# Two late output stores moved from SyncE's queue to GpSimd's queue in a dilated-convolution kernel

## The chip, the cores and the metric

The kernel runs on one core of a Trainium2 chip. The metric is the device time in microseconds of one execution; the median of the runs is compared.

## The reference

A gated causal convolution with three taps and dilation 2, followed by a projection, on `x` of 2 x 16000 x 256, `w` of 3 x 256 x 512 and `w_o` of 256 x 256, all in bf16:

```
xp = jnp.pad(x, ((0, 0), (4, 0), (0, 0)))
h = x @ w[0] + xp[:, 2:2 + T] @ w[1] + xp[:, 0:T] @ w[2]     # taps at t, t-2, t-4
f, g = h[..., :256], h[..., 256:]
z = tanh(f) * sigmoid(g)
out = z @ w_o
```

## The kernel before, in words

Time is cut into groups of rows. A wide group holds 256 rows of 8 time steps (the first wide ones 128 rows), and is worked in four blocks of 128 output channels of `h`. For each block TensorE multiplies sums and differences of shifted inputs with prepared weights (the function `mm`), ScalarE and VectorE put the partial results together, ScalarE takes tanh and sigmoid, VectorE multiplies both to `z`. Then `out_mm` projects a piece of `z` (128 rows, two time steps each, 2 x 256 columns in PSUM), a copy on ScalarE or VectorE brings it to a bf16 tile `osb` in SBUF, and a store takes it to `out`. All this is written out in one order by hand (`tc.manual_schedule()`), so the order of the text is the order on each engine.

In the middle of the kernel two pieces share one store of 256 KB, issued on SyncE's queue by `store` (L391). At the end, from the last four pieces of the group before on, every piece has a store of its own, 128 KB. The last group has eight pieces: (row block 0 or P, jp 0 to 3). `out_mm` writes them into `G["o", rb0, jp]`. `last_evict` (L665) takes two of them: it copies the first with ScalarE and the second with VectorE into the two halves of one `osb`, and issues one store after each copy (L675), on the queue that its argument `queues` names for it. With `split` the second piece is copied in two halves, one on each engine.

In the text below the eight stores at L675 are named by their place: in the order of the program these are N1 and N2 (row block 0, jp 1 and 2, L693), N3 and N4 (row block P, jp 1 and 2, L695), A1 and N5 (row block 0, jp 0 and 3, L696), N6 and A2 (row block P, jp 0 and 3, L699). N1, N3, A1 and N6 follow a copy by ScalarE, N2, N4 and N5 one by VectorE, and A2 the two half copies. A1 and A2 are issued from ScalarE's queue, the six N from SyncE's.

After the last of them SyncE waits at L725 for the completion of all transfers; then the engines meet in a closing barrier.

Of the kernel before, what the change touches and what calls it, by code (L numbers as in the profile page):

```python
# [13 lines left out]
def kernel(  # L14
# [23 lines left out]
    nc = tc.nc  # L38
# [4 lines left out]
    P = 128  # L43
# [621 lines left out]
    def last_evict(rb0, jps, queues, split=False):  # L665
        osb = osb_pool.tile([P, 2, 2, D], bf16, name="osb")
        rows = out[b, t0 + 8 * rb0:t0 + 8 * (rb0 + P), :].rearrange("(p j) d -> p j d", j=8)
        at = [rows[:, 2 * jp:2 * jp + 2, :] for jp in jps]
        for i, (jp, copy) in enumerate(zip(jps, (nc.scalar.copy, nc.vector.tensor_copy))):
            if split and i:  # L670
                for q, half_copy in enumerate((nc.vector.tensor_copy, nc.scalar.copy)):
                    half_copy(out=osb[:, i, q], in_=G["o", rb0, jp][q])  # L672
            else:
                copy(out=osb[:, i], in_=G["o", rb0, jp])  # L674
            queues[i].dma_start(out=at[i], in_=osb[:, i])  # L675

    def last_mm(rb0, jps, where):
        two_pieces([(G, rb0, jp) for jp in jps], where)
# [11 lines left out]
    out_evict(*left[1][0], False, True)  # L690
    out_evict(*left[1][1], False, True)
    last_mm(P, (1, 2), "y")
    last_evict(0, (1, 2), (nc.sync, nc.sync))  # L693
    last_mm(0, (0, 3), "o")
    last_evict(P, (1, 2), (nc.sync, nc.sync))  # L695
    last_evict(0, (0, 3), (nc.scalar, nc.sync))  # L696
    out_mm(G, P, 0, new_y()[:, 0].rearrange("p (q d) -> p q d", q=2))
    out_mm(G, P, 3, [new_y()[:, 0, :D], ps_o.tile([P, D], f32, name="o_ps", tag="o_ps")[:]])
# [31 lines left out]
```

## Time and profile before

| | |
|---|---|
| median of 3 runs | 262.14 us (261.97 to 263.0) |
| the profiled execution: its own time | 261.54 us |
| the profiled execution: its span, first to last instruction | 259.8 us |
| TensorE busy | 254.9 us, 98% of the span |
| VectorE, ScalarE, GpSimd busy | 226.0, 246.1, 115.3 us |
| SyncE's and ScalarE's transfers (q1, q10) | 33.99 and 0.92 MB |

The busy times are sums over the span. In a row of the timeline the first number is the start in us from the span's start and the second the duration; SPq, ACTq and POOLq are the queues of SyncE, ScalarE and GpSimd, and a DMA_DIRECT2D on one of them is the issuing of a transfer, not its data. "DMA share" in a table of stretches is the mean busy share of the core's 16 DMA engines in that stretch, as their packet records give it (it can come out a little over 1).

### The profile page before, as it was taken

What the parts mean: (1) busy time and instruction counts of PE and PEld (TensorE: products, weight loads), DVE (VectorE), ACT (ScalarE), POOL (GpSimd) and SP (SyncE); (2) the same over time, 40 slices, a digit from 0 to 9 for tenths busy, and PEclk for the clock granted to TensorE, in tenths of its full rate; (3) what the DMA queues carried; (4) which work ended last, traced back from release to release, by engine and by line L of the source; (5) the groups of instructions that cost most, each with busy time, mean ns of one, the idle gap of its engine ahead of it and who ended that gap; (6) DMA issues with size and microseconds to landing.
All of it is one profiled execution on the core that took longest, in us unless ns stands there. A gap on an engine that the chain in (4) does not pass through costs nothing.

```text
span 259.8 us, 4299 instructions
## 1 busy us (share of the span) xinstructions
PE 254.9 (98%) x1491; PEld 146.0 (56%) x1491; DVE 226.0 (87%) x270; ACT 246.1 (95%) x378; POOL 115.3 (44%) x128
## 2 busy tenths in 40 slices
PE   8999999999999999999999999999999999999993
PEld 4577765555555555555555555555555555555572
DVE  2889999988988988999988988988988988986673
ACT  5768889999999999999999999999999999999993
POOL 1432435445445445446445445445445445444240
PEclk9999999999999999999999999999999999999999
DMA  7999782471925628283481925728294221221226
GB/s 199 208 196 213 150 203 81 113 207 50 252 81 125 171 85 210 82 178 116 129 208 40 252 83 111 182 87 209 81 153 142 82 81 43 81 83 43 81 101 222
DMA packets 79685, 35.17 MB, mean 135 GB/s; under 512 B 69552, under 2 KB 72368, under 8 KB 79664
## 3 DMA queue, kind: packets, MB, share of 16 engines
q1 hardware_dynamic: 78560, 33.99, 52.1%
q10 hardware_dynamic: 1104, 0.92, 1.4%
q8 instruction: 11, 0.18, 0.3%
q14 instruction: 10, 0.08, 0.1%
HBM read 1.18 MB, written 16.38 MB: 68 GB/s over the span
## 4 chain that ended last, share of the span: by engine, by line
PE 97%; DVE 0%; ACT 0%; issue 0%; DVEq 0%; ACTq 0%
PE y L259 70%; PE o_ps L374 19%; PE y L316 2%; PE e_ps L316 2%; PE y L149 1%; PE y L374 1%; PE f_ps L316 1%; PE wt_ps L170 0%; DVE osb L674 0%; ACT osb L674 0%; PE tp L182 0%; PE tq L182 0%; DVEq L725 0%; ACT osb L672 0%; DVEq L672 0%
## 5 line engine op out<-in xcount | busy, mean ns | idle before, releaser
L293 POOL TENSOR_TENSOR sv<-sv,st 128x512 f32<-128x512 f32 x60 | 76.5, 1275 | 17.4 <-ACT sv L290 7.9
L241 POOL TENSOR_TENSOR qd<-xq 128x256 bf16<-128x256 bf16 (+2 forms) x58 | 33.7, 585 | 111.4 <-DVE zw L349 54.5
L300 DVE TENSOR_TENSOR sv<-sv,y 128x1024 f32<-128x1024 f32 x60 | 72.7, 1212 | 4.0 <-PE y L259 3.8
L259 PE MATMUL y<-qd,wd_sb 128*128 128x512 bf16 (+1 forms) x256 | 61.6, 366 | 0.0
L411 ACT CAST osb<-o_ps 128x512 bf16<-128x512 f32 x114 | 61.1, 591 | 0.0
L374 PE MATMUL o_ps<-wo_sb,zw 128*128 128x256 bf16 x450 | 58.9, 273 | 0.0
L296 DVE SCALAR_TENSOR_TENSOR y<-st,y 128x512 f32<-128x512 f32 x60 | 41.8, 696 | 19.6 <-PE y L259 11.1
L374 PEld LDWEIGHTS <-zw 128*128 128x128 bf16 x480 | 46.9, 98 | 17.4
L259 PE MATMUL y<-qp,wmh_sb 128*128 128x512 bf16 (+1 forms) x128 | 45.0, 366 | 0.0
L259 PEld LDWEIGHTS <-wd_sb 128*128 128x128 bf16 x256 | 25.0, 98 | 27.4 <-issue 0.5
L221 DVE TENSOR_TENSOR q<-xq 128x2048 bf16<-128x2048 bf16 (+3 forms) x34 | 37.9, 1119 | 0.9 <-DMA xq<-in_x_dram 0.8
L290 ACT ACTIVATE sv<-y 128x512 f32<-128x512 f32 x60 | 35.9, 598 | 0.9 <-PE y L259 0.7
L286 ACT ACTIVATE st<-y 128x512 f32<-128x512 f32 x60 | 36.3, 606 | 0.2 <-PE y L259 0.2
L259 PE MATMUL y<-q,wu_sb 128*128 128x512 bf16 (+1 forms) x128 | 35.7, 366 | 0.0
L259 PE MATMUL y<-qm,wph_sb 128*128 128x512 bf16 (+1 forms) x128 | 35.7, 366 | 0.0
L259 PE MATMUL y<-q,wt_sb 128*128 128x512 bf16 (+1 forms) x128 | 35.7, 366 | 0.0
L259 PE MATMUL y<-qm,wm_sb 128*128 128x512 bf16 (+1 forms) x128 | 35.7, 366 | 0.0
L349 DVE TENSOR_TENSOR zw<-thw,sgw 128x2048 bf16<-128x2048 bf16 x28 | 34.1, 1218 | 0.0
L340 ACT ACTIVATE sgw<-sv 128x1024 bf16<-128x1024 f32 x30 | 32.3, 1078 | 0.7 <-DVE sv L300 0.5
L340 ACT ACTIVATE thw<-sv 128x1024 bf16<-128x1024 f32 x30 | 32.3, 1078 | 0.3 <-DVE sv L300 0.3
L340 ACT ACTIVATE sgw<-y 128x1024 bf16<-128x1024 f32 x30 | 31.3, 1044 | 0.0
L340 ACT ACTIVATE thw<-y 128x1024 bf16<-128x1024 f32 x30 | 31.3, 1043 | 0.0
(68 smaller groups left out, 179.9 us busy)
## 6 DMA issues: line engine op xcount, KB each, us to landing
out_dram<-osb SPq DMA_DIRECT2D x54, 256.0 KB, 2.1
out_dram<-osb SPq DMA_DIRECT2D x10, 128.0 KB, 1.9
w_sb<-in_w_dram ACTq DMA_DIRECT2D x2, 256.0 KB, 4.2
out_dram<-osb SPq DMA_DIRECT2D x2, 160.0 KB, 2.0
xq<-in_x_dram SPq DMA_TRANSPOSE x17, 6.7
osb<-in_x_dram SPq DMA_DIRECT2D x1, 256.0 KB, 2.5
w_sb<-in_w_dram SPq DMA_DIRECT2D x1, 256.0 KB, 3.8
out_dram<-osb ACTq DMA_DIRECT2D x2, 128.0 KB, 2.1
```

The lines of the kernel that those rows point to most:

```text
L221: ins = nc.vector.tensor_tensor(out=sums(G, "q")[:, h, :, :, :, sl].rearrange("p h q ct r -> p h (q ct) r"), in0=s, in1=a, op=ALU.subtract ...
L241: ins = after(eng.tensor_tensor(out=sums(G, "qd")[:, h, q, ct, sl], in0=a, in1=s, op=ALU.subtract), behind)
L259: nc.tensor.matmul(B.y[:, bank, i * n:(i + 1) * n], lhsT=wmat[:, ct, osl], rhs=mv[:, :, ct, :B.R], start=new and ct == 0 and i == 0, stop= ...
L286: nc.scalar.mul(B.st[:], B.y[:, 0, :], 4.0)
L290: nc.scalar.mul(B.sv[:, 0], B.y[:, 0, :], 2.0)
L293: after(nc.gpsimd.tensor_tensor(out=B.sv[:, 1], in0=B.sv[:, 0], in1=B.st[:], op=ALU.subtract), behind)
L296: nc.vector.scalar_tensor_tensor(out=B.y[:, 1, :], in0=B.st[:], scalar=-0.5, in1=B.y[:, 0, :], op0=ALU.mult, op1=ALU.add)
L300: nc.vector.tensor_tensor(out=B.sv[:], in0=B.sv[:], in1=B.y[:], op=ALU.subtract)
L340: nc.scalar.activation(out=dst[:, :, ph].rearrange("p b j c -> p j b c"), in_=at[:].rearrange("p j (b c) -> p j b c", b=hi - lo), func=fun ...
L349: return eng.tensor_tensor(out=z, in0=th, in1=sg, op=ALU.mult)
L374: nc.tensor.matmul(o_ps[q] if isinstance(o_ps, list) else o_ps[:, q, :], lhsT=z_columns(G, rb0, jp, q, dt), rhs=wo_sb[:, dt, :], start=(dt ...
L411: copy(out=G["osb"][:, 2 * h:2 * h + 2, :], in_=o_ps)
```

## The change

The first store of two pairs, N1 and N3, is issued from GpSimd's queue. Nothing else is changed in the text.

```diff
     last_mm(P, (1, 2), "y")
-    last_evict(0, (1, 2), (nc.sync, nc.sync))
+    last_evict(0, (1, 2), (nc.gpsimd, nc.sync))
     last_mm(0, (0, 3), "o")
-    last_evict(P, (1, 2), (nc.sync, nc.sync))
+    last_evict(P, (1, 2), (nc.gpsimd, nc.sync))
     last_evict(0, (0, 3), (nc.scalar, nc.sync))
```

On SyncE's queue these rows stand at the end of the last group; DMAHW0 to DMAHW7 are the completion counts that transfers of the two hardware queues take in turn, Activation and DVE the counts of finished instructions of ScalarE and VectorE.

```order
-L675 DMA out_dram<-osb 128x512 [waits DMAHW0_49,Activation_49]
-L675 DMA out_dram<-osb 128x512 [waits DMAHW1_49,DVE_49]
-L675 DMA out_dram<-osb 128x512 [waits DMAHW2_49,Activation_49]
-L675 DMA out_dram<-osb 128x512 [waits DMAHW4_49,DVE_49]
-L675 DMA out_dram<-osb 128x512 [waits DMAHW5_49,DVE_49]
-L675 DMA out_dram<-osb 128x512 [waits DMAHW7_49,Activation_49]
+L675 DMA out_dram<-osb 128x512 [waits DMAHW0_49,DVE_49]
+L675 DMA out_dram<-osb 128x512 [waits DMAHW2_49,DVE_49]
+L675 DMA out_dram<-osb 128x512 [waits DMAHW3_49,DVE_49]
+L675 DMA out_dram<-osb 128x512 [waits DMAHW5_49,Activation_49]
```

The two stores that waited for ScalarE's copies, N1 and N3, are gone; N2, N4, N5 and N6 are left in their order and use the counts one or two places earlier.

On GpSimd's queue this is the end of the program; `sv` and `zw` are the last block's partial sums and gated values.

```order
 L293 TENSOR_TENSOR sv<-sv,st 128x512 [waits Activation_49,Pool_49]
 L644 TENSOR_TENSOR zw<-thw,sgw 128x1024 [waits PE_49]
+L675 DMA out_dram<-osb 128x512 [waits Activation_49] x2
 L725 UNCONDITIONAL_BRANCH
 L725 ISA [waits barrier_Pool_Activation_PE_DVE_SP_gather]
```

The two stores stand behind GpSimd's last arithmetic instruction and ahead of its part of the closing barrier. The order on TensorE and VectorE is the same as before; on ScalarE only the numbers of the counts differ.

## The prediction

> **What bounds the kernel now.** I read the page first: what ends the kernel, and whether the DMA engines matter there.
>
> ```profile
> span 259.8 us, 4299 instructions
> PE 97%; DVE 0%; ACT 0%; issue 0%; DVEq 0%; ACTq 0%
> DMA  7999782471925628283481925728294221221226
> GB/s 199 208 196 213 150 203 81 113 207 50 252 81 125 171 85 210 82 178 116 129 208 40 252 83 111 182 87 209 81 153 142 82 81 43 81 83 43 81 101 222
> ```
>
> TensorE carries 97% of the chain, and the change touches nothing that TensorE waits for: only the last slice (222 GB/s over 6.5 us) can move. Next the issues by line, for the sizes, and the end in stretches, whose last two columns are DMA share and GB/s.
>
> ```profile
> out_dram<-osb SPq DMA_DIRECT2D x10, 128.0 KB, 1.9
> out_dram<-osb ACTq DMA_DIRECT2D x2, 128.0 KB, 2.1
> ...
> 254.00:255.00 1.00, 1.00 (x12) 0.90 (x10) 0.97 (x2) 1.00 (x2) 0.00 (x0) 1.00 0.79 262
> 255.00:256.00 1.00, 0.68 (x7) 0.36 (x4) 1.00 (x3) 0.57 (x3) 0.00 (x0) 1.00 0.82 269
> 256.00:258.00 2.00, 0.00 (x0) 0.00 (x0) 0.21 (x1) 0.34 (x2) 0.00 (x0) 1.00 1.03 340
> 258.00:258.30 0.30, 0.00 (x0) 0.00 (x0) 0.00 (x0) 0.00 (x0) 0.00 (x0) 1.00 0.95 318
> 258.30:259.80 1.50, 0.00 (x0) 0.00 (x0) 0.00 (x0) 0.00 (x0) 0.00 (x0) 1.00 0.01 3
> ```
>
> Two regimes. Until 256.0 the DMA engines have a fifth of their time free (0.79, 0.82). From 256.0 to 258.3 they are full at 340 GB/s, so a store of 128 KB (131,072 bytes) takes 0.386 us there. The rest, 1.5 us, is landing and closing. Now SyncE's queue in that time, from the timeline in narrow windows (start, duration of the issue).
>
> ```profile
> 252.68 1.30 SPq L391 DMA_DIRECT2D out_dram<-osb  x3
> 253.58 0.40 SPq L391 DMA_DIRECT2D out_dram<-osb  x1
> 254.07 0.41 SPq L675 DMA_DIRECT2D out_dram<-osb  x1
> 254.58 0.38 SPq L675 DMA_DIRECT2D out_dram<-osb  x1
> 255.06 0.40 SPq L675 DMA_DIRECT2D out_dram<-osb  x1
> 255.55 0.44 SPq L675 DMA_DIRECT2D out_dram<-osb  x1
> 256.08 0.41 SPq L675 DMA_DIRECT2D out_dram<-osb  x1
> 256.58 0.40 SPq L675 DMA_DIRECT2D out_dram<-osb  x1
> ```
>
> The last six rows are N1 to N6, one about every 0.5 us: 131,072 bytes in 0.5 us are 262 GB/s, the rate of the first regime, which the issuing sets. And the copies that release the stores, with ScalarE's own two issues.
>
> ```profile
> 253.22 0.62 ACT L674 CAST osb<-y 128x512 bf16<-128x512 f32 x1
> 253.97 0.59 ACT L674 CAST osb<-y 128x512 bf16<-128x512 f32 x1
> 255.07 0.36 ACTq L675 DMA_DIRECT2D out_dram<-osb  x1
> 255.48 0.59 ACT L674 CAST osb<-y 128x512 bf16<-128x512 f32 x1 [0.43 <-PE y L374]
> 256.37 0.36 ACTq L675 DMA_DIRECT2D out_dram<-osb  x1
> ...
> 253.86 1.42 DVE L674 CAST osb<-y 128x512 bf16<-128x512 f32 x2 [0.61 <-ACT osb L674]
> 254.59 0.69 DVE L674 CAST osb<-y 128x512 bf16<-128x512 f32 x1
> 255.20 0.68 DVE L674 CAST osb<-o_ps 128x512 bf16<-128x512 f32 x1
> 255.79 0.41 DVE L672 CAST osb<-y 128x256 bf16<-128x256 f32 x1
> ```
>
> N1 is ready at 253.22 + 0.62 = 253.84, N2 at 253.86 + 0.69 = 254.55, N3 at 253.97 + 0.59 = 254.56, N4 at 254.59 + 0.69 = 255.28, N5 at 255.20 + 0.68 = 255.88, N6 at 255.48 + 0.59 = 256.07. SyncE issues them 0.23, 0.03, 0.50, 0.27, 0.20 and 0.51 us later. That is the slack the change is about.
>
> **Why the end stands where it does.** Two more numbers: how long after its issue a store's data move, and what follows the data (the row of landings is that of the eight stores).
>
> ```profile
> 253.40:253.50 0.10, 0.10 (x3) 0.09 (x2) 0.00 (x0) 0.10 (x1) 0.00 (x0) 1.00 0.00 0
> 253.50:253.90 0.40, 0.40 (x6) 0.35 (x5) 0.04 (x1) 0.33 (x1) 0.00 (x0) 1.00 0.89 300
> ...
> DMA to landing us min/median/max: 1.9/2.1/2.4
> ...
> L725 SPq EVENT_SEMAPHORE  x3: 17/17/28, 258.9 to 259.7; - x3
> L725 SPq DRAIN  x3: 7/7/13, 259.0 to 259.3; - x3
> ```
>
> The store issued at 252.68 begins to move data at 253.5: 0.82 us. With that, first data come at 254.89 (N1), 255.40 (N2), 255.88 (N3), 255.89 (A1), 256.37 (N4), 256.90 (N5), 257.19 (A2), 257.40 (N6). N1 and N2 find idle engines. From N3 on, six stores stand back to back: 255.88 + 6 x 0.386 = 258.20, where the table shows the data ending at 258.3. The last landing is taken at 258.9, 0.6 us behind the data, and 0.9 us of closing lead to 259.8. So the kernel's end is the end of this DMA train plus 1.5 us.
>
> **The change part by part.** *SyncE loses two issues.* Nothing queued on it is held any more than by its own copy: N2 goes at 254.58, N4 at 255.30, N5 at 255.91, N6 when N5's 0.41 us and the gap of 0.09 seen between these rows are over, 256.41. Gains: 0, 0.25, 0.17 and 0.17 us. A1 and A2 stay at 255.07 and 256.37. The other completion counts cost nothing: each was last used by a store issued at 252.68 or before (N1 to N6 land 1.9 to 2.4 us after issue), and N6 issues 3.7 us after that.
>
> *What this is worth alone.* First data: N2 255.40, A1 255.89, N4 256.12, N5 256.73, A2 257.19, N6 257.23. If N1 and N3 were out of the way before 255.40, the floor would be A2 and N6 behind 257.19: 257.19 + 2 x 0.386 = 257.96, 0.24 us earlier than 258.20. That is the largest gain there is; the engines are full, and bytes are not removed.
>
> *GpSimd gains two issues.* The trace of before shows no DMA on its queue, so the price g of one is bounded by rows.
>
> ```profile
> 247.69 2.13 POOL L644 TENSOR_TENSOR zw<-thw,sgw 128x1024 bf16<-128x1024 bf16 x1
> ...
> L293 POOL TENSOR_TENSOR sv<-sv,st 128x512 f32<-128x512 f32 x60 | 76.5, 1275 | 17.4 <-ACT sv L290 7.9 <-DVE qm L232 5.5 <-DVE q L221 4.0
> ...
> L446 POOL TENSOR_TENSOR wph_sb<-sv,w_sb 128x1024 bf16<-128x1024 f32 x1 | 3.2, 3162 | 5.1 <-DVE sv L444 5.1
> ```
>
> The queue is free from 249.82 (247.69 + 2.13), 4 us before N1 is ready, so nothing there holds the stores and nothing but the barrier stands behind them. From below, g is SyncE's 0.40 us. From above it is the longest thing GpSimd does here, 3.16 us. I take 1.28 us, its usual price for one instruction on a 128x512 tile, as the nearest row of the same engine and shape; it is a choice, not a measurement. Behind the issue I keep SyncE's 0.82 - 0.40 = 0.42 us to the first data. Then N1 starts at 253.86, its data move at 253.86 + 1.28 + 0.42 = 255.56, and N3, which has been ready since 254.56 but stands behind N1, moves at 253.86 + 2 x 1.28 + 0.42 = 256.84.
>
> *The sum.* N1 now misses the idle time ahead of N2. From N2 on, all eight stores stand in one train without a gap: 255.40 + 8 x 0.386 = 258.49, against 258.20. That is +0.29 us. With g = 0.40, N1 is through at 255.07, N3 comes at 255.40 together with N2, and seven stores follow: 255.40 + 7 x 0.386 = 258.10, so -0.10 us. With g between about 1.1 and 1.5 the train is the same eight, and up to 1.8 a gap of a tenth comes into it; above that N3 itself is last: its landing is 253.86 + 2g + 0.42 + 0.386 + 0.6 = 255.27 + 2g, which reaches today's 258.9 at g = 1.82 and, at g = 3.16, 261.6: +2.7 us.
>
> The Trainium skill, "DMA: Bandwidth & Descriptors", section "Rules for kernel authors", says that transfers issued from SyncE, ScalarE and GpSimd run on the same 16 engines and interleave, so spreading them saves issue time only. The row of 340 GB/s agrees: the full stretch gains nothing from another queue. The page's "Specifications" give about 1 us to the first byte from GpSimd against 0.6 us from SyncE; by that estimate N1 would come 0.4 us later than by SyncE's rows, at 255.08, eight stores would end at 258.17, and the change would be worth nothing.
>
> **The sum against the runs.** On the profiled execution the span goes from 259.8 to 260.1 and its own time from 261.54 to 261.8. The median of the runs shown is 262.14, 0.6 above that execution; on it the forecast is 262.4 us. Half a per cent, 1.3 us, is about what a measurement of this kernel can tell from no change.
>
> **The rivals.** *GpSimd issues nearly as quickly as SyncE* (g up to 0.8). For it: its smallest rows are short and its queue is idle. Against it: no row shows it issuing anything. The time: -0.24 to 0, that is 261.9 to 262.1. Within half a per cent. Chance 0.14.
>
> *GpSimd's stores are slow, and N3 becomes the last to land.* This is the case on the other side: slower. The place is the wait at L725, the price twice g because N3 queues behind N1 on one in-order queue. It is slower by over 1.3 us when 255.27 + 2g exceeds 260.2, from g = 2.47 on, or when the first store, the first that this queue issues in the whole kernel, takes that much extra once. For it: 2.13 and 3.16 us rows on this engine, at double the tile; nothing has been issued there before. Against it: the 60 instructions on this tile's shape take 1.28. The time: 263.4 to 264.8. Chance 0.23.
>
> *VectorE holds GpSimd up while it copies.* VectorE's copies run almost without a break from 253.86 to 255.79 + 0.41 = 256.20. If GpSimd could prepare nothing beside them, both stores would start at 256.20: with g = 1.28 N3's data come at 256.20 + 2.56 + 0.42 = 259.18, end at 259.57, against 258.20: +1.4 us, 263.5; with g = 0.40 five stores from N5's 256.73 on end at 258.66, +0.5 us, 262.6. For it: the kernel itself orders GpSimd's arithmetic behind VectorE's (`after`, L92). Against it: that concerns instructions with two SBUF inputs; these copies have one input, in PSUM. Chance 0.09, half of it over the bound. The Trainium skill, "SBUF — State Buffer", section "SBUF: two separate sides", describes such a hold-up of GpSimd's transfers for VectorE's two-port modes; no run here shows it so far, and by its condition these copies would not cause it.
>
> *A gain of over half a per cent* finds no row: the floor is 0.24 us. I leave 0.03 for what the profile does not show.
>
> **How the numbers follow.** The forecast (g about 0.9 to 2.2, end moved by 0 to +0.8 us) has 0.51. Within half a per cent: 0.51 + 0.14 + 0.04 = 0.69, less 0.03 for runs that scatter upward = 0.66. Slower: 0.23 + 0.05 + 0.03 = 0.31. Faster: 0.03. The range goes from the floor's 261.9 less a tenth for scatter, 261.8, up to g = 3.16, 264.8; below it I leave the 0.03 and some scatter, above it a longer first issue.
>
> **What would show it.** Right: in the timeline N4, N5 and N6 issue on SPq at 255.3, 255.9 and 256.4; two DMA_DIRECT2D on POOLq, the first from 253.86, over 1 us each; the DMA share in 254 to 255 lower than 0.79, then full without a gap until about 258.5; the last landing at 259.2. Wrong: if a stretch with a low DMA share appears after 257 and the wait at L725 ends on one of GpSimd's two stores, the issue was slow (or, if it begins only after 256.2, held up by the copies); if the full stretch ends before 258.2, it was quick. Any difference ahead of 253 us is not from this change.

## The result and the profile after

The changed kernel takes 262.51 us (median of 22 runs, 261.95 to 263.59) against 262.02 us (22 runs, 261.35 to 263.0). The ratio is 1.0023, 95% interval 1.0014 to 1.0033: slower by about 0.6 us by the ratio (0.5 between the medians), inside the half per cent. The forecast was 262.4, the range 261.8 to 264.8.

The profiled execution after has a span of 261.4 us, 1.6 us more, and most of that lies ahead of the change. From the page, the chain of work that ended last:

```profile
span 261.4 us, 4298 instructions
PE 88%; DMA 4%; SPq 4%; issue 1%; DVE 1%; ACT 0%; DVEq 0%; ACTq 0%
```

In this execution the chain runs through waits for loads and through SyncE's queue, which the same instructions did not show before; ScalarE's first copy at L674 starts at 254.29 instead of 253.22. This part scatters from execution to execution (below). So the end is compared as a **tail**: from the start of that copy to the end of the span. It was 6.54 us (253.22 to 259.75, from the unrounded times); it is 261.40 - 254.29 = 7.11, or 0.57 more. To set a time after against one before, subtract 1.07.

The timeline of the tail, in narrow windows: ScalarE's first copy, GpSimd's two issues, SyncE's four (N2, N4, N5, N6), ScalarE's two.

```profile
254.29 1.34 ACT L674 CAST osb<-y 128x512 bf16<-128x512 f32 x2
255.22 0.71 POOL L675 DMA_DIRECT2D out_dram<-osb  x1 [4.32 <-ACT osb L674]
255.94 0.55 POOL L675 DMA_DIRECT2D out_dram<-osb  x1
255.66 0.33 SPq L675 DMA_DIRECT2D out_dram<-osb  x1
256.38 0.33 SPq L675 DMA_DIRECT2D out_dram<-osb  x1
256.98 0.33 SPq L675 DMA_DIRECT2D out_dram<-osb  x1
257.41 0.60 SPq L675 DMA_DIRECT2D out_dram<-osb  x1
256.15 0.36 ACTq L675 DMA_DIRECT2D out_dram<-osb  x1
257.50 0.36 ACTq L675 DMA_DIRECT2D out_dram<-osb  x1
```

N1 is ready at 254.29 + 0.62 = 254.91 (copy's duration as before) and its issue starts 0.31 us later. GpSimd then takes 0.71 us for it and 0.55 for N3. Now the DMA engines, share and GB/s in the last two columns, with one row of before at the matching place (255.02 + 1.07 = 256.09) ahead.

```profile
255.02:255.41 0.39, 0.39 (x7) 0.34 (x4) 0.39 (x2) 0.03 (x1) 0.00 (x0) 1.00 0.90 299
```

```profile
255.50:256.00 0.50, 0.50 (x7) 0.45 (x5) 0.47 (x2) 0.50 (x2) 0.49 (x2) 1.00 0.79 262
256.00:256.10 0.10, 0.10 (x3) 0.09 (x2) 0.10 (x1) 0.10 (x1) 0.10 (x1) 1.00 0.15 41
256.10:256.50 0.40, 0.40 (x7) 0.34 (x4) 0.40 (x2) 0.02 (x1) 0.39 (x1) 1.00 0.00 0
256.50:256.90 0.40, 0.26 (x3) 0.00 (x0) 0.40 (x2) 0.29 (x1) 0.00 (x0) 1.00 1.05 370
256.90:257.30 0.40, 0.00 (x0) 0.00 (x0) 0.39 (x2) 0.40 (x2) 0.00 (x0) 1.00 0.85 258
257.30:257.70 0.40, 0.00 (x0) 0.00 (x0) 0.00 (x0) 0.17 (x1) 0.00 (x0) 1.00 0.76 259
257.70:258.10 0.40, 0.00 (x0) 0.00 (x0) 0.00 (x0) 0.00 (x0) 0.00 (x0) 1.00 0.92 310
258.10:258.50 0.40, 0.00 (x0) 0.00 (x0) 0.00 (x0) 0.00 (x0) 0.00 (x0) 1.00 1.01 333
258.50:259.50 1.00, 0.00 (x0) 0.00 (x0) 0.00 (x0) 0.00 (x0) 0.00 (x0) 0.90 0.99 342
259.50:259.80 0.30, 0.00 (x0) 0.00 (x0) 0.00 (x0) 0.00 (x0) 0.00 (x0) 0.50 0.91 311
259.80:259.90 0.10, 0.00 (x0) 0.00 (x0) 0.00 (x0) 0.00 (x0) 0.00 (x0) 0.50 0.10 21
```

This is the main part: for 0.4 us, from 256.10 to 256.50, the 16 engines move nothing, where before they moved N1. N1's data come a little ahead of N2's, and all eight stores then stand in one train. The train is not full all the way: behind its first 0.4 us the share is 0.85, 0.76 and 0.92 until 258.10, and only then 1. By the packet records (each transfer's pieces, with their times) the data end 5.56 us after the first copy instead of 5.19: 0.38 us later. The rest of the 0.57 is in the closing: first SyncE's waits at L725, the last row of waits before, then after.

```profile
L725 SPq EVENT_SEMAPHORE  x1: 28/28/28, 258.9 to 258.9; - x1
L725 SPq DRAIN  x1: 13/13/13, 259.0 to 259.0; - x1
```

```profile
L725 SPq EVENT_SEMAPHORE  x3: 28/28/28, 260.4 to 260.5; - x3
L725 SPq DRAIN  x1: 13/13/13, 260.6 to 260.6; - x1
```

Before, the wait that N6's landing ended was the last of SyncE's list. Now N6 has an earlier completion count, two more waits stand behind it, at 0.06 us each, and SyncE goes on 0.12 us later. From there to the end of the span it took 0.75 us before and takes 0.81 now. Most of this is in one row of GpSimd's queue, which clears semaphores (the counters that the waits read): before, then after.

```profile
L725 POOLq EVENT_SEMAPHORE_RANGE_CLEAR  x1: 94/94/94, 259.4 to 259.4; - x1
```

```profile
L725 POOLq EVENT_SEMAPHORE_RANGE_CLEAR  x1: 138/138/138, 261.0 to 261.0; - x1
```

It takes 138 or 139 ns in every run below with a store on GpSimd's queue, and 94 to 96 in every run without one.

### The profile page after: what moved, and what is told of

It reads as the page before. It is cut to its first block, busy times and chain, and to the rows that moved or that the text cites. A ratio compares the mean times of both kernels' runs of the same rounds, so it can differ in the third digit from the quotient of the medians.

```text
span 261.4 us, 4298 instructions
## 1 busy us (share of the span) xinstructions
PE 255.9 (98%) x1491; PEld 146.3 (56%) x1491; DVE 225.3 (86%) x270; ACT 246.2 (94%) x378; POOL 116.2 (44%) x130
## 4 chain that ended last, share of the span: by engine, by line
PE 88%; DMA 4%; SPq 4%; issue 1%; DVE 1%; ACT 0%; DVEq 0%; ACTq 0%
PE y L259 67%; PE o_ps L374 19%; DMA xq<-in_x_dram 4%; SPq L128 3%; PE y L374 1%; PE f_ps L316 1%; SPq L114 1%; DVE sv L300 0%; PE e_ps L316 0%; DVE osb L674 0%; ACT osb L674 0%; SPq L145 0%; SPq L141 0%; DVEq L725 0%; ACT osb L672 0%
## 5 line engine op out<-in xcount | busy, mean ns | idle before, releaser
L221 DVE TENSOR_TENSOR q<-xq 128x2048 bf16<-128x2048 bf16 (+3 forms) x34 | 37.2, 1100 | 0.9 <-DMA xq<-in_x_dram 0.9
```

Of the source, the lines that this page charges most:

```text
L221: ins = nc.vector.tensor_tensor(out=sums(G, "q")[:, h, :, :, :, sl].rearrange("p h q ct r -> p h (q ct) r"), in0=s, in1=a, op=ALU.subtract ...
```

## The experiments

Every experiment keeps the kernel's arithmetic and moves stores, or cuts two of them in pieces, and nothing else. "First copy" is ScalarE's first copy at L674. The data end is taken from the packet records, the rest is the tail less the data end.

| kernel | tail us | data end us | rest us | ratio to before (95%) |
|---|---|---|---|---|
| before | 6.54 | 5.19 | 1.35 | |
| before, against itself | 6.54 | 5.20 | 1.35 | 1.0004 (0.9992 to 1.0017) |
| changed | 7.11 | 5.56 | 1.54 | 1.0023 (1.0014 to 1.0033) |
| changed, again | 7.10 | 5.57 | 1.53 | one run |
| changed, a third time | 7.10 | 5.57 | 1.53 | 1.0036 (1.0022 to 1.0051) |
| N1 alone on GpSimd | 6.87 | 5.43 | 1.44 | 1.0001 (0.9984 to 1.0017) |
| N1 alone, again | 6.88 | 5.43 | 1.46 | 1.0016 (1.0006 to 1.0027) |
| N3 alone on GpSimd | 6.67 | 5.27 | 1.40 | 1.0003 (0.9984 to 1.0021) |
| N6 alone on GpSimd | 6.78 | 5.34 | 1.44 | 1.0001 (0.9982 to 1.0020) |
| a store at L391 on GpSimd | 6.62 | 5.17 | 1.45 | 1.0012 (0.9998 to 1.0026) |
| two early stores on GpSimd | 6.70 | 5.19 | 1.50 | 0.9994 (0.9975 to 1.0012) |
| counts shifted, no GpSimd | 6.73 | 5.22 | 1.50 | one run |
| N3 on ScalarE | 6.51 | 5.21 | 1.29 | 1.0021 (1.0007 to 1.0035) |
| N3 on ScalarE, again | 6.51 | 5.22 | 1.28 | 1.0006 (0.9994 to 1.0018) |

The tail repeats within 0.01 us in every pair and triple of the same kernel; the medians scatter by 0.1 to 0.2% around what the tails give. Single edits are therefore judged by their tails.

**N1 alone.**

```diff
-    last_evict(0, (1, 2), (nc.sync, nc.sync))
+    last_evict(0, (1, 2), (nc.gpsimd, nc.sync))
```

> Only N1 goes to GpSimd's queue. The measure is the tail, from the start of ScalarE's first copy at L674 to the span's end: 6.54 us before (253.22 to 259.75), 7.11 us after the change (254.29 to 261.40). Theory M (missed gap): N1's data come so late (1.3 us after the issue) that they miss the idle time ahead of N2, and the last full train has one store more, about 0.4 us; N3 on SyncE is as before. Tail 7.0 to 7.1, the median up by 0.4 to 0.5 us. Rival P (each store issued from GpSimd costs the same share): tail 6.8, median up by 0.25. Rival C (a GpSimd queue in use at the end costs a fixed sum in the closing): tail 7.1, with the data ending 5.2 us after the anchor as before, not 5.6.

Three rows of its table of stretches:

```profile
255.05:255.45 0.40, 0.40 (x7) 0.35 (x4) 0.40 (x2) 0.03 (x1) 0.00 (x0) 1.00 0.00 0
255.45:255.95 0.50, 0.27 (x3) 0.00 (x0) 0.50 (x2) 0.38 (x1) 0.00 (x0) 1.00 0.94 324
255.95:256.45 0.50, 0.00 (x0) 0.00 (x0) 0.30 (x1) 0.48 (x2) 0.00 (x0) 1.00 1.01 326
```

The same empty 0.4 us, with one store moved. But the tail is 6.87, not 7.0 to 7.1: the data end only 0.24 us later. After the hole the engines are nearly full at once (0.94, then 1.01). The matching rows of before:

```profile
255.41:255.91 0.50, 0.27 (x3) 0.00 (x0) 0.50 (x2) 0.43 (x1) 0.00 (x0) 1.00 0.83 266
255.91:256.42 0.51, 0.00 (x0) 0.00 (x0) 0.30 (x1) 0.43 (x2) 0.00 (x0) 1.00 0.90 301
```

There they still had a tenth or more free, so part of the extra store is made up for. M's cause is seen, its size was too large, and by the tail alone rival P (6.8) was nearer. The median said nothing the first time; the second time, 1.0016 agrees with 0.34 us of 262.

**N3 alone.**

```diff
-    last_evict(P, (1, 2), (nc.sync, nc.sync))
+    last_evict(P, (1, 2), (nc.gpsimd, nc.sync))
```

> Only N3 goes to GpSimd's queue. Theory M: N1 and N2 find the idle time as before, N3's data join a train that is full anyway and SyncE's N4 to N6 issue earlier into it, so the data end 5.1 to 5.2 us after the first copy at L674 (5.19 before, 5.56 after the change). Tail 6.6 to 6.7, median up by about 0.1 us, hardly to be told from no change. Rival P: tail 6.8. Rival C: tail 7.1.

```profile
255.63:256.03 0.40, 0.40 (x7) 0.35 (x4) 0.40 (x2) 0.03 (x1) 0.40 (x1) 1.00 0.89 298
```

At the place of the hole the engines are busy (0.89), and the tail is 6.67 as M said, not 6.8. But M had the data ending at 5.1 to 5.2, and they end at 5.27, 0.08 us later than before: N3's store is not free either. The two parts of the change cost 0.24 and 0.08 us of data; together 0.38, so 0.05 or so comes from both being there. It goes with the shares of 0.85, 0.76 and 0.92 behind the hole in the changed kernel, where N1 alone has 1.01; why the engines are not full there was not tried.

**One store two places ahead of N1.**

```diff
-    out_evict(*left[1][0], False, True)
+    out_evict(*left[1][0], False, True, nc.gpsimd)
```

(Not shown: `out_evict` gets one more argument, the queue, and hands it on to `store`.)

> One store goes to GpSimd's queue as in the run with N1 alone, but the one two places earlier (the first of the two stores at L391 ahead of N1, issued 0.11 us ahead of the first copy at L674). N1 to N6 are on SyncE again; completion counts and the closing are those of the run with N1 alone. Theory M (missed gap): this store's data, late by 0.4 us, still find free engines, N1 and N2 too, so the last full train is the one of before: data end 5.2 us after the first copy at L674 (before 5.19, N1 alone 5.43), tail 6.6 (N1 alone 6.87). Rival P (a store from GpSimd costs the same wherever it stands): data end 5.4, tail 6.85. Median up by 0.1 or by 0.3.

Its issue by GpSimd, then the stretch that its late data leave empty, the one in which they come, and the place where N1 alone has its hole:

```profile
254.65 0.71 POOL L391 DMA_DIRECT2D out_dram<-osb  x1 [3.32 <-ACT osb L411]
...
255.52:255.70 0.18, 0.18 (x4) 0.16 (x2) 0.18 (x1) 0.18 (x1) 0.00 (x0) 1.00 0.04 11
...
256.01:256.51 0.50, 0.50 (x7) 0.44 (x6) 0.46 (x2) 0.50 (x2) 0.00 (x0) 1.00 0.98 332
256.51:256.91 0.40, 0.40 (x7) 0.35 (x4) 0.40 (x2) 0.03 (x1) 0.00 (x0) 1.00 0.84 274
```

This is the pair that tells M from P: one store, the same queue, 0.71 us of issuing, the same counts in the closing (rest 1.45 and 1.44), only two places earlier. Data end 5.17 against 5.43. This store leaves the engines empty too, for 0.18 us, where they were busy before (0.91); but behind it they had a fifth free, and they make it up at 0.98 where they ran at 0.80. Here a late store cost nothing in the data because the idle time came ahead of a stretch with room; N1's comes just ahead of the last train. Its median (1.0012, an interval that holds 1) is higher than its tail says; I put no weight on it.

**N6, the last of SyncE's.**

```diff
-    last_evict(P, (0, 3), (nc.sync, nc.scalar), True)
+    last_evict(P, (0, 3), (nc.gpsimd, nc.scalar), True)
```

> Only N6, SyncE's very last store, goes to GpSimd's queue. Theory M: its data come at about 4.4 us after the first copy at L674, while the engines are still full with the others, so the train ends as before, at 5.2: tail 6.6 to 6.7, although the latest store of all is on the slower queue. Rival P: tail 6.8. Rival L (a GpSimd store's longer way to landing, 2.2 to 3.1 us in the profile after against 1.9 to 2.4, is added at the end): tail 7.0 or more.

```profile
258.26:258.76 0.50, 0.00 (x0) 0.00 (x0) 0.00 (x0) 0.00 (x0) 0.00 (x0) 1.00 0.96 313
258.76:259.26 0.50, 0.00 (x0) 0.00 (x0) 0.00 (x0) 0.00 (x0) 0.00 (x0) 0.97 0.81 285
```

A miss for M by 0.1 us: tail 6.78. The packet records give the first data of N6 at 4.81 us after the first copy, not 4.4; the train was running out before it came, and the data end at 5.34. Rival L (7.0) is out; the 2.2 to 3.1 us from issue to landing that it went by are those of all stores in the profile after, and GpSimd's two take 2.4 and 2.6. P's 6.8 fits, and by this run alone P is nearer than M.

**Two early stores.**

```diff
-                nc.sync.dma_start(out=rows[h], in_=osb[h * RE:(h + 1) * RE])
+                nc.gpsimd.dma_start(out=rows[h], in_=osb[h * RE:(h + 1) * RE])
```

> The eight last stores are those of before; the two 64 KB stores of the short end group, far ahead of the end of the kernel, are issued from GpSimd instead. Theory M: data end at 5.2 us after the first copy at L674 as before; what is left is the closing alone, two more waits behind the last landing (about 0.06 us each, since the last store now has another completion count, that SyncE waits for earlier in its list) and some 0.06 us of GpSimd's own closing work: tail 6.6 to 6.75. Rival P (two stores at 0.28 us each) and rival C (the queue in use): tail 7.1.

Data end 5.19 and tail 6.70, as M said: no price of 0.28 us a store, and no fixed 0.57. What is left is 0.16 us of closing. It also answers whether the queue's first issue is a costly one:

```profile
L406 POOL DMA_DIRECT2D out_dram<-osb_end x2: 592/655/718, 57.4 to 58.1; - x2
```

0.72 and 0.59 us, half tiles and 200 us earlier, as 0.71 and 0.55 in the tail: the first is dearer than the one right behind it by 0.13 to 0.16 us, no more.

**Counts shifted, without GpSimd.**

```diff
-                nc.sync.dma_start(out=rows[h], in_=osb[h * RE:(h + 1) * RE])
+                for q in range(2):
+                    for r in range(0, RE, 32):
+                        nc.sync.dma_start(
+                            out=rows[h][r:r + 32, q, :], in_=osb[h * RE + r:h * RE + r + 32, q, :])
```

> No store goes to GpSimd. The two 64 KB stores of the short end group, far ahead of the end, are cut into eight of 16 KB, so that the completion counts of the last stores stand as in the changed kernel: N6 has count 5 of 0 to 7 instead of 7, and two waits on older counts stand behind its wait in SyncE's list. Theory: the order of these waits, not GpSimd's queue, costs 0.12 us of the tail: data end 5.19 as before, tail 6.65. Rival (the closing of GpSimd's queue itself costs all of the 0.16 us that the run with early GpSimd stores showed): tail 6.54.

```profile
L728 SPq EVENT_SEMAPHORE  x3: 28/28/28, 259.9 to 260.0; - x3
L728 SPq DRAIN  x1: 13/13/13, 260.1 to 260.1; - x1
```

The same picture as after: three waits ahead of the drain instead of one. From N6's landing to the end of the drain it takes 0.22 us, as after, where it took 0.10 before. So 0.12 us of the change's price has nothing to do with GpSimd's queue: the number of hardware-queue transfers in the whole program sets here which wait is last. (With N1 alone or the store at L391 on GpSimd's queue the counts move by one place, and one wait stands behind N6's instead of two.) The tail, 6.73, is 0.08 us over the 6.65 that was expected: the data end 0.04 us later than before, and N6 lands 0.03 us later behind them; why is not known. From the drain on it takes 0.75 us as before, so the rest of 1.50 is the same as with early GpSimd stores by chance: there the landing comes sooner and GpSimd's closing is longer.

**N3 on ScalarE's queue.**

```diff
-    last_evict(P, (1, 2), (nc.sync, nc.sync))
+    last_evict(P, (1, 2), (nc.scalar, nc.sync))
```

> Only N3 leaves SyncE, and ScalarE issues it. Theory M: the store comes at the hardware queues' price, 0.9 us from issue to data, about 0.5 us earlier than from SyncE, so it fills the free time behind N2 and seven stores follow N2: data end 2.26 + 7 x 0.41 = 5.1 us after the first copy at L674, nothing added in the closing: tail 6.45. ScalarE pays 0.36 us of issuing ahead of A1's copy, and A2, the last copy, may come 0.1 to 0.3 us later: then 6.5 to 6.7. Rival (taking stores off SyncE does not matter at all, the engines are full): data end 5.2, tail 6.54 or more.

The tail, 6.51, is 0.03 us under before, at the lower end of the 6.5 to 6.7 named for a late A2; the data end at 5.21, not 5.1. A1's copy and ScalarE's later ones start about 0.55 us later, which probably gives back what the earlier issue brought. The median of 1.0021 did not fit the tail, so this kernel was run again beside the kernel before against itself and the changed kernel.

> N3 on ScalarE's queue, again, on the same chip. By its tail (6.51 against 6.54) it is the same as the kernel before, ratio 1.000; by the first median it is 0.2% slower. If 1.002 comes again, something ahead of the tail pays for the edit that the tail does not show.

> The kernel before, unchanged, against itself: what a difference of medians is worth here, and the tail before once more. Ratio 1.000; tail 6.54 as in the first profile. If the ratio of this pair comes out off 1 by 0.1 to 0.2%, medians of that size (N3 on ScalarE: 1.0021 with a tail of 6.51) say nothing about an edit.

The second time N3 on ScalarE is 1.0006, within the interval of no change, and the kernel before against itself 1.0004. The 1.0021 did not come again; what made it is not known. No kernel tried here is faster than the one before.

**The changed kernel and N1, again.**

> The changed kernel once more, for how well the tail repeats. If the tail is a property of the program and the differences ahead of it are scatter, it is 7.1 again (7.11 in the profile after) within 0.05 us, whatever the span; if the tail scatters by some tenths, the comparisons of single tails say little.

> The changed kernel on the same chip as the kernel before against itself. Theory M with the closing: tail 7.10, so 0.57 us more, ratio 1.002. If the difference of the medians were mostly scatter ahead of the tail, the ratio would lie anywhere within 0.999 to 1.001.

> N1 alone on GpSimd, again, on the same chip: tail 6.87 as before, so 0.33 us or 0.13% over the kernel before; the first runs of it gave 1.0001 with an interval of 0.0017 either way.

Spans of 261.4, 261.9 and 260.1 us, tails of 7.11, 7.10 and 7.10: what moves a single execution by a microsecond and more lies ahead of the tail. The ratios 1.0023 and 1.0036 have overlapping intervals, and 0.57 us of 262, 1.0022, lies in both (at the edge of the second).

## Why the prediction was right

**The place and the regime: right.** The tail's 0.57 us account for the ratio's 0.6, so no more than the last 7 us need have moved by the change; and no freed issue slot paid (N3 on ScalarE's queue, too, gains only 0.03 us of tail).

**SyncE's gain: right, and worthless as it stood.** N4, N5 and N6 were forecast at 255.30, 255.91 and 256.41; less 1.07 they go at 255.31, 255.91 and 256.34.

**The price of GpSimd's issue: wrong by half, and made good by a term that was left out.** g was chosen as 1.28 us; it is 0.71 and 0.55. The prediction let the issue start 0.02 us behind the copy, and it starts 0.31 behind; it kept 0.42 us from the end of the issue to the first data, and they come 0.58 and 0.92 us after it (the records give 1.29 and 1.47 us from the start). So N1's data come at 255.44 in before's time, where 255.56 was forecast, and N3's at 256.34 instead of 256.84. With the true g and the other two terms as they stood, N1 would have come at 254.99, in the idle time, and N3 at 255.54; seven stores from 255.40 on would have given -0.10 us. That N1 missed the idle time as forecast is luck in this term: two errors of opposite sign nearly met.

**The train of eight: right, but not without a gap.** It was to start with N2 and end 0.29 us later than before; it ended 0.38 us later. By the packet records it takes 3.35 us for eight stores, 0.42 a store, not the 0.386 of the full stretch. Before, it was not six full stores from N3 on but seven from N2 on, at the same 0.42 us (2.92 us, with shares of 0.83 and 0.90 at first), and it ended at 258.40, not 258.20. So the step is one store of 0.42 us, less 0.05 for the train's earlier start.

**The closing: missing.** The prediction held that other completion counts cost nothing, and looked only at whether a count was still in use. Their order in SyncE's list costs 0.12 us, and GpSimd's own closing about 0.06. With 0.38 this makes 0.56 of the 0.57 of the tail.

**The size: half.** The forecast step was +0.3 us, the tail's is 0.57. The number 262.4 stands so near 262.51 also because it was set on a median of three runs, 262.14, where 22 runs have 262.02.

**The signs.** SyncE's three issues came where they were named, there is no low share after 257, and the last landing is at 259.3 in before's time (259.2 was named). GpSimd's issues of over 1 us did not come, the low share stands behind 255.0 and not ahead of it, and the stretch behind it is not without a gap.

**The rivals.** The quick queue (g up to 0.8) was right about g and wrong about the time, for the 0.31 us ahead of the issue and the longer way behind it. The slow queue is out: 0.71 us is the first issue. A hold-up by VectorE's copies is not seen: GpSimd issued N1 in 0.71 us from 255.22 on, beside VectorE's copies (254.94 on), and N6, in its own run, in the same 0.71 us with VectorE idle (behind the stretch's length stand the busy times of TensorE, its weight loads, VectorE, ScalarE and GpSimd):

```profile
257.21:257.92 0.71, 0.00 (x0) 0.00 (x0) 0.00 (x0) 0.00 (x0) 0.71 (x1) 1.00 1.01 343
```

The Trainium skill, "SBUF — State Buffer", section "SBUF: two separate sides", ties such a hold-up to VectorE's two-port modes; that these copies, out of PSUM, show none agrees with it. The estimate from the Trainium skill, "DMA: Bandwidth & Descriptors", section "Specifications", 0.4 us more to the first byte, fits N1 from the start of its issue on: 1.29 us to the first data, where SyncE's N1 and N2 took 0.93 and 0.90 before (GpSimd's other stores took 1.45 to 1.65). What it lacked is the 0.3 us ahead of the issue: from ready to first data GpSimd took 1.6 us for N1, SyncE 0.93 for N2 before.

## What to carry to other kernels

No run here shows a moved store that helped. By these traces it could help only if it was late for its queue and reached the DMA engines while they had room; here the first moved store was hardly late (0.23 us behind its copy) and came 0.4 us later by GpSimd, leaving the engines empty just ahead of a train that they could not shorten. Look at the DMA share by stretches before choosing which store may be slow. For effects of half a microsecond in a kernel that scatters by nearly two, compare the tail from a fixed instruction in the traces, not the spans.

## What the runs showed of the hardware

- A 128 KB store from GpSimd's queue: its issue starts 0.29 to 0.31 us behind the copy that releases it, takes 0.71 us (0.55 for the one that followed at once), and the first data move 1.29 to 1.65 us after the issue's start, against 0.83 to 0.93 for SyncE's stores up to N2 before, whose engines had room.
- It moves in 32 packets of 4096 bytes (160 to 207 ns each), where SyncE's and ScalarE's stores of this size move 128 of 1024 bytes (44 ns and more, mostly 46 to 51). In the changed kernel, where GpSimd's store and N2 move together, A1 on ScalarE's queue waits 1.43 us for its first data instead of 0.88 (1.39 with N1 alone); the cause was not tried.
- The closing's clearing of semaphores takes 0.14 us instead of 0.09 when GpSimd's queue issued a store anywhere in the kernel.
- SyncE's last issue took 0.60 us in all three profiles of the changed kernel (0.60 to 0.61), 0.40 before; its cause was not tried.
